# Pooled attention with a frequency mix on one core: the maxima row as a 128x32 product, the tail maxima's last columns at the second burst, and a new order of the first pair

## The chip, the core and the metric

The kernel runs on one core of a Trainium2 chip. The metric is device microseconds of one execution. Engines are named as in the profile: PE (TensorE), DVE (VectorE), ACT (ScalarE), POOL (GpSimd), SP (SyncE, which issues most transfers); PEld is PE's loading of stationary tiles.

## The reference

Inputs: `q`, `k`, `v` of 8 batches x 8 heads x 1152 rows x 64, and four weights. Cut to what is computed:

```python
q_pool = q.reshape(B, H, S // 2, 2, D).mean(axis=3)
scores = scale * q_pool @ k^T
attn = exp(scores - rowmax(scores)); attn = attn / (rowsum(attn) + 1e-9)
x = (attn @ v), heads side by side             # 8 x 576 x 512
theta = x @ w_theta
y = w_tok_r @ (x * cos(theta)) + w_tok_i @ (x * sin(theta))
u = x + y
out = u + max(u @ w_ch, 0)
```

## The kernel before, in words

Two heads are one pair; 32 pairs run one after the other, and then 8 batches of the second phase (theta, cosine and sine, token mix, channel mix).

For each pair, `q` and `k` are loaded (`load_q`, `load_k`, L468 and L478), neighbouring q rows are added (`pool_q`, L484), turned on DVE (`turn_q`, `turn_k`), and split into a rounded part `hi` and a rest `lo`. Pair 0 has its own way: `load_first` (L449) and `first_prep` (L532) turn on PE and copy out of PSUM. A first pass over the pair (`maxpass`, L578) multiplies only the rounded parts, in 12 blocks `pm`, named by two digits (`pm_00` to `pm_32`), each reduced on DVE to row maxima (L599). The last 64 pooled rows of both heads, the tail, take a product of their own with 128x128 tiles: 128 columns in one of the 12 blocks (L596, the block that TAIL_IN names) and 1024 columns in `max_tail` (`px`, L612). `max_nm` folds the maxima (L624), `max_row` (L626) turns them into 9 rows on PE, `max_copy` and `load_max` bring them to the operand `nmr`.

Then 18 score blocks (`escore`, L656), two halves u of 9 K tiles: eight products `pe` in 64x128 tiles, and an exponential on ACT into a buffer `pc`. POOL adds the `pc` tiles up (`ssum`, L679). Two bursts per pair (`burst`, L765) multiply `pc` with `v` (`av`, L702, tile `pa`, 128x64 tiles). The first burst ends with the maxima row of the next pair and the row sums of the last (`norm_sum`, L725, 128x32 tiles); the second begins with `max_tail` for the pair after next.

PSUM has four double banks. `bank2` hands out the one that was given back longest ago, so every product waits for the reader of the block that had its bank before.

The order on every engine is written out by hand. Each step has a position, 18 for each pair and one for each score block, from the tables at the top of the file (EARLY for pairs 0 to 2, MAX_AT0 to MAX_AT2 for their maxima, PLAN, AV_AT and others for the rest, X0_DN and X0_SC for the first batch's normalisation, and for the second phase positions of 56 for each batch, SC1_AT and STORE_LAG among them). The steps are sorted by position, and each engine runs its instructions in that order. `xscale` (L247) multiplies a quarter of x with the reciprocal sums that `dload` brought; `xload` brings x back from memory (DRAM); `zrest` (L402) is the subtraction that gives a rest Z; `fstore` (L1202) writes results out; `xnload` (L263) brings rows of x.

Of the kernel before, what the change touches and what calls it, by code (L numbers as in the profile page):

```python
# [10 lines left out]
F32 = mybir.dt.float32  # L11
F32R = mybir.dt.float32r
# [3 lines left out]
ALU = mybir.AluOpType  # L16
# [4 lines left out]
SHORT = (2, 3, 5, 7, 9, 11, 15, 16, 17, 21, 23, 28, 30)  # L21
REST = (3, 6, 9, 12, 15, 18)
WHOLE = ()
WARM = 16
AGAIN = ((3, 3, 3, 3, 3, 3, 3, 3, 3, 5, 3, 3), (3, 2, 1, 1, 1, 1, 1, 1, 1, 1, 1, 1))
PC_BUFS = 14
MAX_A = ((-23.16, -21.04, -20.44, -19.56, -18.24, -16.98), (-23.16, -21.62, -20.02, -18.45, -18.24, -16.98))
# [3 lines left out]
G_AT = 3.88  # L31
SS_LAG = 6.079
AV_AT = (10.348, 19.269)
AV_AT0 = (10.348, 19.269)
# [4 lines left out]
ROUND1 = (-21.9, -21.8, -21.7)  # L39
LOADV = (-58.9, 11)  # L40
TAIL_IN = (3, 2)
EARLY = {
    0: dict(load_first=-70, first_prep=-60, tail=-25.8, round_lo=-25.75, max=-20.5),
    1: dict(load_k=-69.5, load_q=-69, pool_q=-59, turn_k=-59.5, turn_q=-23.8, tail=-21.65, round_lo=-21.6, max=10.35),
    2: dict(load_k=-58.96, load_q=-58.95, pool_q=-1.0, turn_q=10.31, turn_k=10.32, round_hi=10.5, tail=10.51, round_lo=13.2),
    3: dict(load_k=10.4, load_q=-0.95),
}
MAX_AT0 = (-25.7, -25.2, -24.7, -24.2, -23.7, -23.2, -22.7, -22.2, -21.9, -21.5, -21.4, -21.3)
MAX_AT1 = (-17.75, -17.7, -16.7, -15.7, -14.7, -13.7, -12.7, -11.7)
MID = ((0, 0, 0), (0, 0, 2),(0,0,4),(0,0,6))  # L50
MAX_AT2 = (-22.5, -21.7, -21.1, -19.5, -18.5, -16.8, -15.5, -13.5, -12.5, -10.5, -9.5, -7.8)
HALF_AT = (-21.6, -21.45)
NM_AT = (0.2, 13)
ROW_AT = (0.7, 13)
# [69 lines left out]
def pooled_attention_moe_kernel(  # L124
# [291 lines left out]
    with ExitStack() as p1:  # L416
# [115 lines left out]
        def first_prep(i):  # L532
            st = state[i]
            raw = st["kb"] = opd.tile([P, S + SQ], F32, tag="lo", name="raw0")
            prep(0)
            qx = [st["qn"][0:QP, :, x].rearrange("p t h d -> p t (h d)") for x in range(2)]
            qp = qx[0]
            nc.vector.tensor_tensor(qp, qx[0], qx[1], ALU.add)
            ta, tb = bank2("pta"), bank2("ptb")
            for t in range(KT):  # L540
                dst = ta[:, t // 4, t % 4 * P : (t % 4 + 1) * P] if t < 8 else tb[:, 0, 0:P]
                nc.tensor.transpose(
                    out=dst, in_=st["kn"][:, t].rearrange("p h d -> p (h d)"), identity=ident
                )
# [3 lines left out]
            parts = (
                (ta.rearrange("p b (t f w) -> p (b t) f w", f=32, w=4), 0, 8),
                (tb[:, 0, 0:P].rearrange("p (t f w) -> p t f w", f=32, w=4), 8, 9),  # L550
                (tb[:, 0, P:].rearrange("p (t f r) -> p t f r", t=4, r=3), 0, 4),
                (tb[:, 1, 0 : 2 * QP].rearrange("p (t f r) -> p t f r", t=2, r=3), 4, 6),
            )
# [53 lines left out]
        def max_tail(i):  # L607
            st = state[i]
            hi, tl = st["hi"], st["tail"]
            pm = st["px"] = bank2(f"px{i}")  # L610
            for n in range(2):
                nc.tensor.matmul(  # L612
                    pm[:, n], tl, hi[:, 512 * n : 512 * (n + 1)], start=True, stop=True
                )
        def max_tail_red(i):
            st = state[i]
            mx = st["mx"]
            nc.vector.tensor_reduce(mx[:, 8, 0:2], st["px"], AX.X, ALU.max)
            done(f"px{i}")
# [436 lines left out]
    with ExitStack() as p2:  # L1056
# [157 lines left out]
        for b in range(B):  # L1214
# [104 lines left out]
```

## Time and profile before

| | us |
|---|---|
| median of 3 runs | 1275.29 |
| lowest and highest | 1274.76, 1275.31 |
| the profiled execution | 1278.34 |
| its span, first to last instruction | 1276.6 |
| mean granted TensorE clock | 0.991 of full |

The profile comes from one execution. Busy time and span are read against each other; the granted clock is 1.00 at 2.4 GHz and 0.50 at 1.2 GHz. A timeline row has start, duration, engine, line, operation, output and inputs with the number of instructions merged into it, and in square brackets the idle time of the engine before it with what ended that.

### The profile page before, as it was taken

The numbers are of one execution on the slowest core, as the hardware profiler recorded it, in microseconds if no ns is written. First come the engines' busy times: TensorE is split into PE (matmuls) and PEld (weight loads), VectorE is DVE, ScalarE is ACT, GpSimd is POOL, SyncE is SP. The second block draws the span as 40 slices with busy tenths as digits, with TensorE's granted clock in tenths as the row PEclk, the third lists the DMA queues.
The fourth block names the chain that finished last, engine by engine and source line by source line (L and its number), as shares of the span: only waits on it lengthen the run. The fifth ranks groups of instructions, "written<-read, shape, count | busy, mean of one in ns | idle before, by whom it ended". The sixth has DMA issues, their size and how long they took to land.

```text
span 1276.6 us, 29050 instructions
## 1 busy us (share of the span) xinstructions
PE 1246.7 (98%) x11556; PEld 1006.2 (79%) x11556; DVE 903.5 (71%) x1173; ACT 696.2 (55%) x1241; POOL 854.1 (67%) x581
## 2 busy tenths in 40 slices
PE   7999999999999999999998999989999999999998
PEld 6677776777777777677776777679999999998998
DVE  5787777877778787788886885486675757657642
ACT  3577576666757667666765566554333433334320
POOL 4799899899899979999998887432423514242410
PEclk8999999999999999999999999989999999999999
DMA  9564565566446456565637511126554464555421
GB/s 125 97 124 99 112 120 78 121 110 106 97 96 120 89 122 102 95 127 97 115 69 157 92 44 45 52 71 179 93 139 89 118 148 82 123 95 136 87 38 38
DMA packets 468660, 129.09 MB, mean 101 GB/s; under 512 B 438390, under 2 KB 438780, under 8 KB 468524
## 3 DMA queue, kind: packets, MB, share of 16 engines
q1 hardware_dynamic: 465728, 126.03, 49.7%
q8 instruction: 91, 1.49, 0.5%
q10 hardware_dynamic: 2572, 0.86, 0.3%
q0 software_dynamic: 224, 0.33, 0.1%
q14 instruction: 45, 0.37, 0.1%
HBM read 96.58 MB, written 29.55 MB: 99 GB/s over the span
## 4 chain that ended last, share of the span: by engine, by line
PE 76%; DVE 5%; DMA 5%; POOL 4%; SPq 4%; ACT 3%; issue 3%; ACTq 0%; DVEq 0%; POOLq 0%
PE pe L673 22%; PE pa L708 20%; PE pf L1099 13%; PE pf L1146 5%; PE pf L326 5%; PE pm L587 4%; POOL ss L688 4%; PE pn L737 3%; ACT pc L676 2%; DMA dn<-rd 2%; PE px L612 2%; SPq L463 1%; DVE xT L250 1%; SPq L1207 1%; DMA xs<-dn 1%
## 5 line engine op out<-in xcount | busy, mean ns | idle before, releaser
L688 POOL TENSOR_TENSOR ss<-ss,pc 128x576 f32<-128x576 f32 x346 | 531.2, 1535 | 50.4 <-ACT pc L676 27.8
L599 DVE TENSOR_REDUCE mx<-pm 128x2 f32<-128x768 f32 x384 | 353.1, 952 | 148.1 <-PE pm L587 144.9
L676 ACT ACTIVATE pc<-pe 128x576 f32<-128x576 f32 x576 | 350.3, 651 | 64.4 <-PE pe L673 35.2
L708 PE MATMUL pa<-pc,vn 128*64 128x288 f32 x2304 | 294.4, 409 | 0.0
L708 PEld LDWEIGHTS pa<-pc,vn 128*64 128x64 f32 x2304 | 159.4, 137 | 116.1 <-issue 7.3
L1099 PE MATMUL pf<-wtk,Z 128*128 128x288 f32 x1728 | 234.9, 296 | 4.4 <-DVE Z L406 3.5
L1099 PEld LDWEIGHTS pf<-wtk,Z 128*128 128x128 f32 x1728 | 232.6, 189 | 6.4 <-DVE Z L406 3.7
L406 POOL TENSOR_TENSOR Z<-ab,Z 128x512 fp32r<-128x512 f32 x35 | 47.1, 1347 | 265.9 <-ACT Z L400 228.1
L673 PE MATMUL pe<-hi 64*128 64x288 f32 x1152 | 198.4, 340 | 6.0 <-DVE mx L599 4.6
L673 PE MATMUL pe<-hi,lo 64*128 64x288 f32 x1152 | 170.9, 292 | 0.0
L673 PE MATMUL pe<-lo,hi 64*128 64x288 f32 x1152 | 170.9, 293 | 0.0
L673 PE MATMUL pe<-nmr,oner 64*128 64x288 f32 x1152 | 170.4, 291 | 0.0
L673 PEld LDWEIGHTS pe<-hi 64*128 64x128 f32 x1152 | 108.3, 184 | 60.3 <-issue 27.6
L587 PE MATMUL pm<-hi 64*128 64x384 f32 x826 | 134.5, 349 | 4.7 <-ACT hi L558 1.6
L720 ACT COPY xu<-pa 128x288 f32<-128x288 f32 x64 | 25.5, 399 | 186.5 <-PE pa L708 153.7
L673 PEld LDWEIGHTS pe<-lo,hi 64*128 64x128 f32 x1152 | 109.6, 186 | 0.0
L673 PEld LDWEIGHTS pe<-hi,lo 64*128 64x128 f32 x1152 | 109.1, 185 | 0.0
L673 PEld LDWEIGHTS pe<-nmr,oner 64*128 64x128 f32 x1152 | 109.0, 185 | 0.0
L1146 PE MATMUL pf<-us,wch 128*128 128x288 f32 x768 | 105.4, 296 | 0.9 <-DVE uT L1113 0.9
L1146 PEld LDWEIGHTS pf<-us,wch 128*128 128x128 f32 x768 | 104.0, 188 | 2.8 <-issue 1.3
L688 POOL TENSOR_TENSOR ss<-pc,pc 128x576 f32<-128x576 f32 x62 | 100.7, 1624 | 0.4 <-ACT pc L676 0.4
L587 PEld LDWEIGHTS pm<-hi 64*128 64x128 f32 x826 | 79.4, 191 | 9.7 <-DVE mx L599 2.5
(165 smaller groups left out, 1476.3 us busy)
## 6 DMA issues: line engine op xcount, KB each, us to landing
vn<-in_v_dram SPq DMA_DIRECT2D x128, 144.0 KB
kn<-in_k_dram SPq DMA_DIRECT2D x124, 144.0 KB
qn<-in_q_dram SPq DMA_DIRECT2D x124, 144.0 KB
xd<-xu SPq DMA_DIRECT2D x32, 288.0 KB
xT<-xd SPq DMA_DIRECT2D x8, 1152.0 KB
out_dram<-ot SPq DMA_DIRECT2D x112, 72.0 KB
xn<-xs SPq DMA_DIRECT2D x31, 256.0 KB
dn<-rd SPq DMA_DIRECT2D x32, 160.0 KB
```

The costliest lines, as they stand in the source:

```text
L326: nc.tensor.matmul(th, xs[:, c, j * P : (j + 1) * P], ws[:, c], start=(n == 0), stop=(n == 11))
L406: eng.tensor_tensor(Z[1], t, Z[0].bitcast(F32), ALU.subtract)
L587: nc.tensor.matmul(pm[:, h, 0:W], hi[hs, Q0 + j * P : Q0 + (j + 1) * P], hi[hs, g * W : (g + 1) * W], start=True, stop=True,)
L599: nc.vector.tensor_reduce(mx[:, j : j + 5 : 4, g : g + 1], pm[:, :, 0:W], AX.X, ALU.max)
L612: nc.tensor.matmul(pm[:, n], tl, hi[:, 512 * n : 512 * (n + 1)], start=True, stop=True)
L673: nc.tensor.matmul(pe[:, h, 0:HALF], w[hs], x[hs], start=(n == 0), stop=(n == 3))
L676: nc.scalar.activation(pcs[u, kt], pe[:, :, 0:HALF], AF.Exp, scale=SC)
L688: nc.gpsimd.tensor_tensor(st["ss", u], first, st["pc"][u, kt], ALU.add)
L708: nc.tensor.matmul(pa[hs, 0, 0:HALF], st["vn"][:, h, kt, :], st["pc"][u, kt][:, h, :], start=(kt == 0), stop=(kt == KT - 1),)
L737: nc.tensor.matmul(px[a : a + 32, 1, 0:HALF], ones, sets[u][n][:, h, :], start=(n == 0), stop=(n == len(sets[0]) - 1), tile_position=(0, a),)
L1099: nc.tensor.matmul(st["py", c, u][:, 0:HALF], Z[zi][:, c * P : (c + 1) * P], wtk[wi][:, kw, u * HALF : (u + 1) * HALF], start=(i == 0 and ...
L1146: nc.tensor.matmul(st["pr", e][u][:, 0:HALF], wch[wi][:, c, e * P : (e + 1) * P], st["us", ui, c // 2][:, c % 2, u * HALF : (u + 1) * HALF ...
```

## The change

`max_row` becomes an ordinary product with a tile position; in the second burst `pa`'s bank is taken after `px`'s; the tail's 128 columns move from block `pm_32` to block `pm_12`, which stands before `max_tail`. Pair 0's loads, copies and order are written anew, pair 0's v comes in one transfer, and 11 instead of 16 warm-up products run. Positions around the end of the attention phase and of the stores move. The core of the diff, the tables cut to the lines that the prediction speaks of:

```diff
-WARM = 16
+WARM = 11
-TAIL_IN = (3, 2)
+TAIL_IN = (1, 2)
 EARLY = {
-    0: dict(load_first=-70, first_prep=-60, tail=-25.8, round_lo=-25.75, max=-20.5),
-    1: dict(load_k=-69.5, load_q=-69, pool_q=-59, turn_k=-59.5, turn_q=-23.8, tail=-21.65, round_lo=-21.6, max=10.35),
+    0: dict(load_first=-70, first_prep=-60, tail=-28.757, round_lo=-29.225, max=-20.74),
+    1: dict(load_k=-65.772, load_q=-66.05, pool_q=-27.673, turn_k=-21.464, turn_q=-22.174, tail=-19.658, round_lo=-2.892, max=10.879),
...
-X0_DN = (0.1, 0.2, 9.3, 18.3)
-X0_SC = (6.088, 15.05, 25.552, 42.088)
+X0_DN = (0.1, 0.2, 15.2, 23.2)
+X0_SC = (13.05, 21.05, 30.05, 42.088)
-SC1_AT = -8.365
+SC1_AT = -7.9
-STORE_LAG = 3.237
+STORE_LAG = (3.237, 3.237, 13.0, 13.0)
...
         def load_first():
             kn = vnp.tile([P, KT, 2, D], F32, tag="vn", name="kn0")
-            qn = inp.tile([P, QT, 2, 2, D], F32, tag="qn", name="qn0")
-            for h in range(2):
-                nc.sync.dma_start(kn[:, :, h], k[0, h].rearrange("(p t) d -> p t d", t=KT))
-                nc.scalar.dma_start(
-                    qn[0:QP, :, :, h], q[0, h].rearrange("(p t x) d -> p t x d", t=QT, x=2)
-                )
+            qn = inp.tile([P, 2, QT, 2 * D], F32, tag="qn", name="qn0")
+            ksrc = k[0, 0:2].rearrange("h (p t) d -> h p t d", t=KT)
+            qsrc = q[0, 0:2].rearrange("h (f r t x) d -> r f h (t x d)", r=3, t=QT, x=2)
+            qdst = [qn[32 * r : 32 * r + 32].rearrange("f h t y -> f h (t y)") for r in range(3)]
+            nc.sync.dma_start(kn[:, :, 0], ksrc[0])
+            nc.scalar.dma_start(qdst[0], qsrc[0])
+            nc.sync.dma_start(kn[:, :, 1], ksrc[1])
+            nc.scalar.dma_start(qdst[1], qsrc[1])
+            nc.sync.dma_start(qdst[2], qsrc[2])
...
             for dst in (st["hi"], raw):
-                kd_ = dst[:, 0:S].rearrange("p (t w f) -> p t f w", t=KT, w=4)
-                qd_ = dst[:, Q0:].rearrange("p (r t f) -> p t f r", r=3, t=QT)
-                for n, (src, t0, t1) in enumerate(parts):
-                    nc.scalar.copy((kd_, qd_)[n // 2][:, t0:t1], src)
+                qd_ = dst[:, Q0:].rearrange("p (r t f) -> p t r f", r=3, t=QT)
+                for n, (src, sl) in enumerate(parts):
+                    to = dst[:, sl] if n < 2 else qd_[:, sl]
+                    if n and dst is not raw:
+                        nc.vector.tensor_copy(to, src)
+                    else:
+                        nc.scalar.copy(to, src)
...
         def max_row(i, px):
-            nc.tensor.transpose(out=px[0:KT, 1, 0:P].bitcast(F32R), in_=state[i]["nm"], identity=identr)
+            nc.tensor.matmul(
+                px[0:KT, 1, 0:P], state[i]["nm"], identr, start=True, stop=True, tile_position=(0, 0)
+            )
...
         def burst(i, u):
-            pa = bank2(f"pa{i}_{u}")
             whole_sum(i - 1 + u, 1 - u)
             if u == 0:
-                av(i, u, pa)
+                av(i, u, bank2(f"pa{i}_{u}"))
                 if i > 0:
                     norm_sum(i - 1, bank2(f"pn{i}"))
             else:
                 if i + 2 < NPAIR:
                     max_tail(i + 2)
+                pa = bank2(f"pa{i}_{u}")
+                if i + 2 < NPAIR:
                     max_tail_red(i + 2)
                 av(i, u, pa)
...
             for e in range(0 if last else ND):
                 at2(base + FLIP_AT[e], flip, b, e)
-                at2(base + FLIP_AT[e] + STORE_LAG, fstore, b, e)
+                at2(base + FLIP_AT[e] + STORE_LAG[e], fstore, b, e)
```

Line numbers of the changed kernel are larger by 2 to 16. Three places of the order, first PE at the two bursts. `pm_32` is the last score block of a pair's maxima, `pa_0` the first burst's tile. Before:

```order
1217 L673 MATMUL pe_11_4314<-nmr_146,oner 128x288 x2
1218 L587 MATMUL pm_31_4325<-hi_3941 128x384 x2
1219 L587 MATMUL pm_32_4329<-hi_3941 128x384 x2
1220 L596 MATMUL pm_32_4329<-hi_3941,tail_151 128x128
1221 L708 MATMUL pa_0_4337<-pc_00_4130,vn_4092 64x288 x2
```

Now, at the same burst:

```order
1218 L688 MATMUL pe_11_4310<-nmr_146,oner 128x288 x2
1219 L600 MATMUL pm_31_4321<-hi_3937 128x384 x2
1220 L600 MATMUL pm_32_4325<-hi_3937 128x384 x2
1221 L723 MATMUL pa_0_4331<-pc_00_4124,vn_4086 64x288 x2
1222 L723 MATMUL pa_0_4331<-pc_01_4138,vn_4086 64x288 x2
```

and at the second burst of that pair, where `pm_12` was followed by `px` directly:

```order
1284 L600 MATMUL pm_12_4514<-hi_4304 128x384 x2
1285 L609 MATMUL pm_12_4514<-hi_4304,tail_150 128x128
1286 L625 MATMUL px_4527<-hi_4304,tail_150 128x512 x2
1287 L723 MATMUL pa_1_4530<-pc_10_4292,vn_4086 64x288 x2
1288 L723 MATMUL pa_1_4530<-pc_11_4309,vn_4086 64x288 x2
```

The product with the tail has gone from behind `pm_32` to between `pm_12` and `px`. The second place is DVE at the first scaling of batch 0's x (`xT`), in pairs 26 and 27. Before:

```order
609 L624 TENSOR_REDUCE nm_10388<-mx_10084 128x9
610 L574 TENSOR_TENSOR lo_10362<-kb_10181,hi_10361 128x1728
611 L250 TENSOR_TENSOR xT_10281<-xT_10281,dn_0_10284 128x640
612 L599 TENSOR_REDUCE mx_10458<-pm_00_10459 128x2
613 L599 TENSOR_REDUCE mx_10458<-pm_01_10489 128x2
```

Now:

```order
612 L637 TENSOR_REDUCE nm_10382<-mx_10078 128x9
613 L587 TENSOR_TENSOR lo_10358<-kb_10175,hi_10357 128x1728
614 L612 TENSOR_REDUCE mx_10451<-pm_00_10452 128x2
615 L612 TENSOR_REDUCE mx_10451<-pm_01_10479 128x2
616 L612 TENSOR_REDUCE mx_10451<-pm_02_10499 128x2
617 L612 TENSOR_REDUCE mx_10451<-pm_10_10528 128x2
618 L612 TENSOR_REDUCE mx_10451<-pm_11_10532 128x2
619 L250 TENSOR_TENSOR xT_10277<-xT_10277,dn_0_10280 128x640
```

The scaling moved behind five reductions of the next pair. The third place is DVE at the start of the second phase, where `Z_7` is a rest that batch 0's token mix needs and `xT`, `dn` and `xl` belong to batch 1. Before:

```order
725 L375 TENSOR_TENSOR ti<-xn,ti 128x512
726 L250 TENSOR_TENSOR xT_12342<-xT_12342,dn_0_12351 128x576 x2
727 L250 TENSOR_TENSOR xT_12342<-xT_12342,dn_2_12356 128x576 x2
728 L406 TENSOR_TENSOR Z_7_12497<-ti,Z_7_12496 128x512
729 L270 STREAM_TRANSPOSE dn_0_12351<-xT_12342 128x512 x2
```

Now:

```order
728 L375 TENSOR_TENSOR ti<-xn,ti 128x512
729 L406 TENSOR_TENSOR Z_7_12491<-ti,Z_7_12490 128x512
730 L250 TENSOR_TENSOR xT_12336<-xT_12336,dn_0_12345 128x576 x2
731 L250 TENSOR_TENSOR xT_12336<-xT_12336,dn_2_12350 128x576 x2
732 L270 STREAM_TRANSPOSE dn_0_12345<-xT_12336 128x512 x2
```

`Z_7` stands ahead of the four scalings now.

## Rows read from the trace of the kernel before

**Rows 1.** The page, busy us of each engine, share of the span, instructions.

```profile
PE 1246.7 (98%) x11556; PEld 1006.2 (79%) x11556; DVE 903.5 (71%) x1173; ACT 696.2 (55%) x1241; POOL 854.1 (67%) x581
```

**Rows 2.** Timeline, the start: start us, us, engine line op out<-in, count [idle].

```profile
9.39 1.94 ACT L558 CAST hi<-pta 128x1024 fp32r<-128x1024 f32 x1 [5.55 <-PE pta L542]
12.26 1.33 PE L587 MATMUL pm<-hi 64*128 64x384 f32 x12 [1.60 <-ACT hi L558]
13.29 1.38 DVE L518 STREAM_TRANSPOSE kb<-kn 128x1152 f32<-128x1152 f32 x1 [3.27 <-DMA kn<-in_k_dram]
14.59 3.52 DVE L599 TENSOR_REDUCE mx<-pm 128x2 f32<-128x768 f32 x4
...
19.16 0.78 DVE L522 STREAM_TRANSPOSE kb<-qp 128x576 f32<-128x576 f32 x1 [1.05 <-POOL qp L489]
...
26.24 0.96 DVE L599 TENSOR_REDUCE mx<-pm 128x2 f32<-128x768 f32 x1 [0.85 <-PE pm L587]
...
28.67 1.21 DVE L618 TENSOR_REDUCE mx<-px 128x2 f32<-128x1024 f32 x1
```

**Rows 3.** Timeline of PE, the first burst of pair 13.

```profile
363.47 0.33 PE L596 MATMUL pm<-hi,tail 128*128 128x128 f32 x1
363.73 4.59 PE L708 MATMUL pa<-pc,vn 128*64 128x288 f32 x36
368.25 0.23 PE L627 MATMUL pa<-identr,nm 128*9 128x128 f32 x1
368.40 0.69 PE L737 MATMUL pn<-ss,ones 128*32 128x288 f32 x8
```

**Rows 4.** Timeline of PE, pair 0's first burst, entered from a score block.

```profile
39.23 0.29 PE L673 MATMUL pe<-nmr,oner 64*128 64x288 f32 x2
...
39.45 0.71 PE L708 MATMUL pa<-pc,vn 128*64 128x288 f32 x4
```

**Rows 5.** Timeline, PE and DVE at the second burst of pair 12.

```profile
351.62 0.34 PE L587 MATMUL pm<-hi 64*128 64x384 f32 x2
...
352.01 0.73 PE L612 MATMUL px<-hi,tail 128*128 128x512 f32 x2
...
349.11 2.68 DVE L599 TENSOR_REDUCE mx<-pm 128x2 f32<-128x768 f32 x3
```

**Rows 6.** DVE's timeline in pairs 26 and 27; busy time, clock and DMA by stretch.

```profile
685.58 3.14 DVE L574 TENSOR_TENSOR lo<-kb,hi 128x1728 fp32r<-128x1728 f32 x1
694.21 0.83 DVE L250 TENSOR_TENSOR xT<-xT,dn 128x640 f32<-128x640 f32 x1 [5.49 <-DMA nmr<-mT]
...
699.09 1.82 DVE L599 TENSOR_REDUCE mx<-pm 128x2 f32<-128x768 f32 x2 [1.16 <-PE pm L587]
...
670.40:723.79 53.39, 49.57 (x523) 36.70 (x522) 38.56 (x40) 29.11 (x55) 47.57 (x32) 0.97 0.64 130
723.79:772.96 49.17, 48.79 (x530) 35.38 (x529) 36.98 (x40) 28.95 (x54) 40.58 (x27) 1.00 0.25 58
```

**Rows 7.** Timeline and stretch at the second phase's start (PE, PEld, DVE, ACT, POOL, clock).

```profile
856.11 6.06 PE L1099 MATMUL pf<-wtk,Z 128*128 128x288 f32 x28 [3.47 <-DVE Z L406]
...
858.39 2.45 DVE L305 TENSOR_TENSOR xl<-xT,xh 128x512 fp32r<-128x512 f32 x4
...
856.10:860.40 4.30, 4.29 (x18) 4.29 (x19) 4.30 (x8) 0.01 (x1) 0.00 (x0) 0.50 0.50 78
```

**Rows 8.** Waits over the span: us in total, times, longest us.

```profile
DVE kk L383 <- DMA xn<-xs: 5.3, 2, 3.3
...
ACT pc L676 <- POOL ss L688: 3.5, 10, 1.3
...
PEld px L612 <- ACT pc L676: 10.9, 30, 0.4
```

**Rows 9.** Transfers between 2.4 and 7.4 us.

```profile
DMA packets 4484, 1.13 MB, mean 227 GB/s; under 512 B 4484, under 2 KB 4484, under 8 KB 4484
```

**Rows 10.** The stretch of pair 21, columns as in rows 6 and 7.

```profile
546.20:570.40 24.20, 24.08 (x266) 17.63 (x262) 19.37 (x23) 17.28 (x32) 23.65 (x16) 1.00 0.64 109
```

More of the change, by code (lines that the diff above doesn't have):

```diff
@@ L33 @@
 AV_AT = (10.348, 19.269)
-AV_AT0 = (10.348, 19.269)
+AV_AT0 = (10.997, 19.1)
 W_SLOTS = ((2.7077, 'F'), (2.7082, 'G'), (9.553, 'G'), (9.5535, 'S'), (10.1975, 'G'), (10.3446, 'T'), (10.3451, 'A'), (10.8111, 'D'), (10.975, 'D'), (19.0577, 'F'), (19.0582, 'D'), (19.0587, 'D'))
@@ L38 @@
 POOL_V = (5, 6, 11, 13, 15, 19, 20, 22, 28, 31)
-ROUND1 = (-21.9, -21.8, -21.7)
-LOADV = (-58.9, 11)
-TAIL_IN = (3, 2)
+ROUND1 = (-21.726, -20.451, -15.632)
+LOADV = (-60.841, 10.654)
+TAIL_IN = (1, 2)
 EARLY = {
-    0: dict(load_first=-70, first_prep=-60, tail=-25.8, round_lo=-25.75, max=-20.5),
-    1: dict(load_k=-69.5, load_q=-69, pool_q=-59, turn_k=-59.5, turn_q=-23.8, tail=-21.65, round_lo=-21.6, max=10.35),
-    2: dict(load_k=-58.96, load_q=-58.95, pool_q=-1.0, turn_q=10.31, turn_k=10.32, round_hi=10.5, tail=10.51, round_lo=13.2),
-    3: dict(load_k=10.4, load_q=-0.95),
-}
-MAX_AT0 = (-25.7, -25.2, -24.7, -24.2, -23.7, -23.2, -22.7, -22.2, -21.9, -21.5, -21.4, -21.3)
-MAX_AT1 = (-17.75, -17.7, -16.7, -15.7, -14.7, -13.7, -12.7, -11.7)
+    0: dict(load_first=-70, first_prep=-60, tail=-28.757, round_lo=-29.225, max=-20.74),
+    1: dict(load_k=-65.772, load_q=-66.05, pool_q=-27.673, turn_k=-21.464, turn_q=-22.174, tail=-19.658, round_lo=-2.892, max=10.879),
+    2: dict(load_k=-55.676, load_q=-63.943, pool_q=-4.606, turn_q=7.314, turn_k=8.538, round_hi=9.549, tail=11.548, round_lo=10.935),
+    3: dict(load_k=10.803, load_q=-9.799),
+}
+MAX_AT0 = (-27.018, -25.789, -25.538, -24.906, -24.391, -22.506, -22.456, -22.091, -21.99, -21.491, -21.3, -21.113)
+MAX_AT1 = (-22.101, -17.248, -16.865, -15.788, -14.814, -13.69, -12.081, -8.94)
 MID = ((0, 0, 0), (0, 0, 2),(0,0,4),(0,0,6))
[L51 to L54, printed above, removed]
+MAX_AT2 = (-21.234, -20.605, -19.611, -18.864, -17.2, -16.832, -15.264, -11.416, -10.736, -9.135, -7.866, -7.72)
+HALF_AT = (-21.576, -21.125)
+NM_AT = (-20.052, 11.601)
+ROW_AT = (1.049, 13.548)
 PLAN = {
@@ L494, in load_v @@
             vn = vnp.tile([P, 2, KT, D], F32, tag="vn", name=f"vn{i}")
+            if i == 0:
+                src = v[b, h0 : h0 + 2].rearrange("h (p t) d -> p h (t d)", t=KT)
+                nc.sync.dma_start(vn.rearrange("p h t d -> p h (t d)"), src)
             src = v[b, h0 : h0 + 2].rearrange("h (f w t) d -> w f h (t d)", w=4, t=KT)
-            for w in range(4):
+            for w in range(4 if i else 0):
                 dst = vn[32 * w : 32 * w + 32].rearrange("f h t d -> f h (t d)")
@@ L535, in first_prep @@
             prep(0)
-            qx = [st["qn"][0:QP, :, x].rearrange("p t h d -> p t (h d)") for x in range(2)]
-            qp = qx[0]
-            nc.vector.tensor_tensor(qp, qx[0], qx[1], ALU.add)
+            qx = [st["qn"][0:QP].rearrange("p h t (x d) -> x p t h d", x=2)[x] for x in range(2)]
+            qp = inp.tile([P, QT, 2, D], F32, tag="kb", name="qp0")
+            nc.vector.tensor_tensor(qp[0:QP], qx[0], qx[1], ALU.add)
             ta, tb = bank2("pta"), bank2("ptb")
@@ L546, in first_prep @@
                 dst = tb[:, t // 4, (t // 4 == 0) * P + t % 4 * QP :][:, 0:QP]
-                nc.tensor.transpose(out=dst, in_=qp[:, t], identity=ident[0:QP, 0:QP])
+                nc.tensor.transpose(
+                    out=dst,
+                    in_=qp[0:QP, t].rearrange("p h d -> p (h d)"),
+                    identity=ident[0:QP, 0:QP],
+                )
             parts = (
[L549 to L552, printed above, removed]
+                (ta.rearrange("p b c -> p (b c)"), slice(0, 8 * P)),
+                (tb[:, 0, 0:P], slice(8 * P, S)),
+                (tb[:, 0, P:].rearrange("p (t r f) -> p t r f", t=4, r=3), slice(0, 4)),
+                (tb[:, 1, 0 : 2 * QP].rearrange("p (t r f) -> p t r f", t=2, r=3), slice(4, 6)),
             )
             for dst in (st["hi"], raw):
-                kd_ = dst[:, 0:S].rearrange("p (t w f) -> p t f w", t=KT, w=4)
-                qd_ = dst[:, Q0:].rearrange("p (r t f) -> p t f r", r=3, t=QT)
-                for n, (src, t0, t1) in enumerate(parts):
-                    nc.scalar.copy((kd_, qd_)[n // 2][:, t0:t1], src)
+                qd_ = dst[:, Q0:].rearrange("p (r t f) -> p t r f", r=3, t=QT)
[5 more added lines that the diff above has]
+                        nc.scalar.copy(to, src)
             done("pta")
@@ L626, in max_row @@
         def max_row(i, px):
-            nc.tensor.transpose(out=px[0:KT, 1, 0:P].bitcast(F32R), in_=state[i]["nm"], identity=identr)
+            nc.tensor.matmul(
+                px[0:KT, 1, 0:P], state[i]["nm"], identr, start=True, stop=True, tile_position=(0, 0)
+            )
         def max_copy(i, px):
```

## The prediction

> **What bounds the kernel now.** I read the page's busy shares first. TensorE (PE) is busy 98% of the span, and no other engine over 71% [rows 1]. So time falls only where PE's own row of work gets shorter or where one of its few stops goes. I then looked for both. The timeline of the start shows PE held by ScalarE's copies and VectorE (DVE) busy with the wrong thing [rows 2]. The timeline of one burst shows what a change of tile shape on PE costs [rows 3 to 5]. The stages around the end of the attention phase show two stops, at 692 and at 852 us [rows 6, 7]. Last I read the lists of waits [rows 8].
>
> The profiled execution took 1278.34 us (span 1276.6), 3.05 above the median of the runs shown, 1275.29. The savings below are read in the profiled execution and taken off the median unchanged.
>
> **Start of pair 0.** The first loads move 1.13 MB at 227 GB/s, all of it in packets under 512 B [rows 9]; half of that, 2.5 us, is q. Now q comes in runs of 3072 B. I take 0.6 us (ends: nothing, and half of q's time, 1.25). The first score block begins at 12.26, released by ScalarE, whose first copy alone took 1.94 with a scattered destination [rows 2]. Now the copies are contiguous or nearly so, and three of the four `hi` copies go to DVE. They still wait for q's transposes, so I take 0.5 (ends: nothing, 1.2). DVE spent 13.29 to 14.67 on pair 1's K transposition before it could begin the maxima at 14.59 [rows 2]. Without that they could begin when the first six products are done, at about 12.95 (half of a row of 1.33 that starts at 12.26). That is 1.6 us; the 1.38 is put back later in the same row of DVE work, so 0.2 stays. Between 14.59 and the end of the last reduction at 29.88 DVE stood idle 1.05 (for pooled q of pair 1 from POOL) and 0.85 (for PE) [rows 2], and another 0.40 that I leave out. The new order puts that q transposition three reductions later, and puts the eleventh block of maxima ahead of the small product that waits for the half row; I count 1.7 of the 1.9 as gone. Sum 3.0 us. POOL now subtracts `lo` of pair 0 before it pools q; that is no cost as long as the pooled q arrives by DVE's new place for it. Ends 0.5 and 4.5: against it stands that in pair 0 the 3 us subtraction for pair 2 is now ahead of the last four maxima of pair 1, and PE's `pm_32` waits for a bank behind them.
>
> **Tail columns moved from the first burst to the second.** In the first burst of a pair PE goes from 64x128 tiles to one 128x128 product (L596), then to 128x64 tiles. The product starts at 363.47 and the first `pa` at 363.73, so 0.26 us pass before `pa` [rows 3]. With the product gone, PE changes directly from 64x128 to 128x64. That change stands in the trace: the last score product starts at 39.23 and `pa` at 39.45, 0.22 us [rows 4], so the direct change is no dearer than the one before the product. Of 32 moved products 1 is in pair 0 (counted with the start) and 10 are followed by 128x128 transposes of a weight tile, which have the same shape as the product; I count nothing for those. 21 x 0.26 = 5.5 us (ends: 21 x 0.18 = 3.8 if the direct change costs 0.08 more; 8.1 if the ten save as much).
>
> In the second burst the product comes in front of `px`, which has its shape and its stationary tile. Before, `px` started 0.39 after the score product [rows 5], and it was waiting for a bank that ScalarE's exponential gives back, 30 times, 10.9 us in all [rows 8]. The change takes `px`'s bank first and `pa`'s second, so `px` gets the bank of an older maximum. In the pair shown DVE is done with that at 349.11 + 2.68 = 351.79, before the old start at 352.01 [rows 5]. So the tail takes the place of a wait. At worst the product starts as late as `px` did and `px` 0.26 after it, which costs 30 x 0.26 = 7.8 us; at best the product starts 0.22 in, as `pa` did at 39.45, and `px` straight behind it, a gain of 30 x 0.17 = 5.1. The truth should lie near 0.22 plus the part of 0.26 that is no change of shape, about where `px` starts now. I take 0. DVE reduces the same number of columns. Only the 0.28 us tail maximum is now ahead of `px`'s, where a 4.6 us burst covers it.
>
> **The maxima row as a 128x32 product.** The transpose starts at 368.25 and the first row sum at 368.40 [rows 3]: 0.15 us, 30 times, 4.5 us in all. It has a shape of its own between 128x64 and 128x32. As a 128x32 product it shares the shape of the sums, but the first sum uses the same 32 columns and must follow it. I take half, 2.3 us (ends 4.5, and a loss of 1.0 if the sums' other three column groups now start later). The Trainium skill, "TensorE: Matmul & The Clock Gate", section "The mechanism", says that a weight load overlaps running products only when the row group differs. All row groups are the same here, so by that rule the first sum's load would still stand open and the whole term would be nearly 0. No row here tells load from drain at 368.25, so the trace neither agrees nor disagrees, and it stays a rival.
>
> **The stop at 692 us.** DVE reached the first scaling of x at 688.7 and stood until 694.21 for its data, and everything behind it on DVE, PE's bank among it, stood too. Pairs 26 and 27 take 53.39 us, the next two 49.17, so 4.2 us are lost, part of it at the lower granted clock (0.97 on the mean) [rows 6]. The scaling now comes five reductions later. In the old trace the fifth ends at 699.09 + 1.82 = 700.91 [rows 6]; less 4.2 that is 696.7, still 2.5 us behind the data. The loads that must wait for it on SP's queue were moved behind it too, one v load ahead of them. I take 4.2 (ends 3.0, 4.8).
>
> **The stop at 852 us.** PE waits 3.47 us until 856.11 for one subtraction on DVE that stands behind four scalings, and then runs 4.30 us at a granted clock of 0.50, the lower level [rows 7]. With the subtraction first, PE goes on at about 852.5. But the scalings, the transposes and the subtractions `xl` follow, and those end some 0.8 us later than 858.39 + 2.45 = 860.84; the next theta product needs them, so PE stops there instead. Theta ended at about 864.8 and would end at 863.0; if the clock falls there once more, all of that is given back. I take 1.2 (ends: 0.5 lost, 3.5 gained).
>
> **Stores.** DVE waits twice, 5.3 us, for `xn` rows that were queued behind eight output stores on SP [rows 8]. The load now goes ahead of them. PE hardly stops there, so I take 0.7 (ends 0, 1.9). The stores end later, but their buffer is not written again for about ten steps. Fewer warm-up products (11 for 16) I cost at nothing, because they end before the loads do.
>
> **Sum.** 3.0 + 5.5 + 0 + 2.3 + 4.2 + 1.2 + 0.7 = 16.9 us: 1278.34 becomes 1261.4, and 1275.29 becomes **1258.4**.
>
> **Rivals.** (a) The row product saves nothing: 1258.4 + 2.3 = 1260.7. For it, the rule above; chance 0.13. (b) PE gets ahead and POOL or DVE becomes the bound, so that what the bursts save (7.8) is taken back: 1266.2. For it, POOL is busy 23.65 of 24.20 us in pair 21 [rows 10]; against it, ScalarE waited for a buffer from POOL only ten times, 3.5 us [rows 8]. Chance 0.10. (c) The new first order stalls in pair 0, on DVE's subtraction ahead of the maxima, and the start gives nothing: 1261.4. Chance 0.14. (d) Slower: `px` waits in every second burst for DVE's maximum of the older block. It decides from 0.65 us per burst (30 x 0.65 = 19.5 us, 16.9 + 2.6), and gives 1278 and more. In the row shown DVE is free 0.2 us before `px` [rows 5], so 0.03. (e) The order does not move what it should and all stays: 1275; 0.02. The forecast has the remaining 0.58.
>
> **Numbers.** A measurement of this kernel can tell about 0.2%, 2.6 us, from no change. (a), (b), (c) and the forecast are all faster by more: 0.95; I move 0.01 of it to no change, for mixtures of bad ends. So faster 0.94, within 0.2% 0.03, slower 0.03. The range takes the forecast's ends (8 us below, if bursts, row and start all reach their good ends) and (a) to (c) on the other side: 1251 to 1267.
>
> **What would show it.** Right: the last reduction of pair 0's maxima starting at about 25.7 instead of 28.67; pair length in the middle 24.2 to 24.4 where it was 24.6; in the first burst `pm` then `pa` with 0.2 to 0.3 us between; no stop near 692; PE going on at 852.5. Wrong: PE rows of L625 released by DVE, ScalarE waiting for POOL in many pairs, or a new stop of over 1 us in pair 0.

## The result and the profile after

| | before | changed |
|---|---|---|
| median of 4 runs, us | 1275.30 | 1262.17 |
| lowest and highest, us | 1274.76, 1277.31 | 1262.05, 1263.99 |
| profiled execution, us | 1278.34 | 1263.99 |

The ratio is 0.9898 (95% interval 0.988 to 0.9915): 13.1 us less, where 16.9 were forecast. Runs of one kernel lie up to 5.3 us apart (the kernel before, beside e1 to e4: 1274.71 to 1280.05), so below, a difference of medians under about 3 us is read only together with a trace. The kernel before ran again beside every set of experiments, with medians from 1275.64 to 1276.59; the ratios are taken against these, so the ratios show 0.5 to 1.6 us less than the medians do.

The page of the changed kernel, the line that answers to [rows 1]. PE has lost 6 us of work and is still the bound:

```profile
PE 1240.7 (98%) x11546; PEld 1002.6 (79%) x11546; DVE 900.7 (71%) x1176; ACT 692.0 (55%) x1238; POOL 852.5 (68%) x581
```

Its timeline at the start, for [rows 2]:

```profile
8.98 1.01 ACT L571 CAST hi<-pta 128x1024 fp32r<-128x1024 f32 x1 [6.03 <-PE pta L548]
...
10.77 1.02 DVE L569 CAST hi<-ptb 128x128 fp32r<-128x128 f32 x3 [0.92 <-PE ptb L553]
...
11.67 5.79 PE L600 MATMUL pm<-hi 64*128 64x384 f32 x36 [0.94 <-DVE hi L569]
...
13.04 5.67 DVE L612 TENSOR_REDUCE mx<-pm 128x2 f32<-128x768 f32 x6 [1.25 <-PE pm L600]
...
26.23 1.21 DVE L631 TENSOR_REDUCE mx<-px 128x2 f32<-128x1024 f32 x1
```

The copy takes 1.01 instead of 1.94, the maxima begin at 13.04 instead of 14.59, and the reduction behind `px` comes at 26.23 instead of 28.67. Pair 1's first score product starts at 51.88, 2.71 us earlier than before (54.59).

The first burst of pair 13, for [rows 3]:

```profile
358.16 0.54 PE L600 MATMUL pm<-hi 64*128 64x384 f32 x4
358.63 4.59 PE L723 MATMUL pa<-pc,vn 128*64 128x288 f32 x36
363.15 0.23 PE L640 MATMUL pa<-identr,nm 128*9 128x128 f32 x1
363.30 0.69 PE L752 MATMUL pn<-ss,ones 128*32 128x288 f32 x8
```

The tail product is gone from here. The maxima row still stands 0.15 us ahead of the first sum, as before, and the profile still calls it 128*9.

Two second bursts, for [rows 5], first that of pair 12, then that of pair 16 with DVE's rows:

```profile
347.06 0.33 PE L609 MATMUL pm<-hi,tail 128*128 128x128 f32 x1
347.22 0.68 PE L625 MATMUL px<-hi,tail 128*128 128x512 f32 x2
...
442.69 0.33 PE L609 MATMUL pm<-hi,tail 128*128 128x128 f32 x1
443.07 0.73 PE L625 MATMUL px<-hi,tail 128*128 128x512 f32 x2
443.73 0.46 PE L723 MATMUL pa<-pc,vn 128*64 128x288 f32 x2
...
441.19 1.82 DVE L612 TENSOR_REDUCE mx<-pm 128x2 f32<-128x768 f32 x2 [0.32 <-PE pm L600]
```

In pair 12 `px` follows the tail product after 0.16 us. In pair 16 it follows after 0.38, just behind the end of DVE's reduction (441.19 + 1.82 = 443.01), whose bank it has. Of the 29 second bursts after 60 us, 11 look like that of pair 16. They belong to 11 of the 12 pairs in the table LATE (L29), for which some blocks of maxima stand later.

The end of the attention phase: DVE at the first scaling, and the stretch of pairs 26 and 27 for [rows 6], with the columns of rows 6 and 7:

```profile
687.86 1.82 DVE L612 TENSOR_REDUCE mx<-pm 128x2 f32<-128x768 f32 x2 [0.34 <-PE pm L600]
689.60 1.02 DVE L250 TENSOR_TENSOR xT<-xT,dn 128x640 f32<-128x640 f32 x1
...
664.12:713.27 49.15, 48.22 (x522) 35.16 (x520) 35.38 (x39) 28.99 (x55) 47.32 (x32) 1.00 0.70 142
```

The scaling does not wait, and pairs 26 and 27 take 49.15 us instead of 53.39. The start of the second phase, for [rows 7]:

```profile
845.38 1.12 PE L326 MATMUL pf<-wth,xh 128*128 128x512 f32 x4
848.31 2.60 PE L326 MATMUL pf<-wth,xl 128*128 128x512 f32 x4 [1.82 <-DVE xl L305]
850.71 1.91 PE L326 MATMUL pf<-wth,xh 128*128 128x512 f32 x4
...
848.30:853.90 5.60, 5.38 (x17) 3.86 (x18) 4.61 (x10) 1.83 (x3) 0.00 (x0) 0.70 0.75 119
```

The stop of 3.47 us is gone, and as the prediction said PE stops at `xl` instead, 1.82 us, with the granted clock at 0.70 on the mean of the stretch behind it. From the lists of waits, for [rows 8]: the wait of `kk` for `xn` (5.3 us before) has left the list, but `ab` waits for `xn` once, 2.7 us, which it did not before. ScalarE waits less for POOL, and the last line is the wait of `px` for an older maximum.

```profile
DVE ab L375 <- DMA xn<-xs: 2.7, 1, 2.7
...
ACT pc L691 <- POOL ss L703: 1.1, 5, 0.4
...
PEld px L625 <- DVE mx L612: 2.5, 13, 0.3
```

Followed through the trace, the lead over the kernel before is 2.71 us at pair 1, 6.29 at pair 26, 10.51 at pair 28, 11.06 at the first product of the second phase, 12.03 at batch 1, and 14.36 at batch 6, the end of what is gained. Pairs 1 to 25 take 24.49 us on the mean where they took 24.63; the prediction's sign was 24.2 to 24.4.

### The profile page after: what moved, and what is told of

Its sections match the earlier page's. It is cut to its first block, busy times and chain, and to the rows that moved or that the text cites. A ratio compares the mean times of both kernels' runs of the same rounds, so it can differ in the third digit from the quotient of the medians.

```text
span 1262.2 us, 29058 instructions
## 1 busy us (share of the span) xinstructions
PE 1240.7 (98%) x11546; PEld 1002.6 (79%) x11546; DVE 900.7 (71%) x1176; ACT 692.0 (55%) x1238; POOL 852.5 (68%) x581
## 4 chain that ended last, share of the span: by engine, by line
PE 89%; DVE 6%; ACT 2%; DMA 1%; issue 1%; POOL 0%; SPq 0%; ACTq 0%; DVEq 0%; POOLq 0%
PE pe L688 26%; PE pa L723 23%; PE pf L1115 16%; PE pf L1162 7%; PE pf L326 6%; PE pm L600 5%; PE pn L752 3%; DVE mx L612 2%; PE px L625 1%; DVE xT L250 1%; PE pm L609 1%; DMA dn<-rd 1%; ACT pc L691 1%; DMA qn<-in_q_dram 1%; PE pq L326 0%
```

## The experiments

Every kernel starts from the changed one. Medians stand beside its 1262.17, ratios beside its 0.9898 (0.0010 of a ratio is 1.3 us).

**e1_row_back.** The row is a transpose again.

```diff
-            nc.tensor.matmul(
-                px[0:KT, 1, 0:P], state[i]["nm"], identr, start=True, stop=True, tile_position=(0, 0)
-            )
+            nc.tensor.transpose(out=px[0:KT, 1, 0:P].bitcast(F32R), in_=state[i]["nm"], identity=identr)
```

> The changed kernel with the maxima row as a transpose again. Theory: the row product saves nothing, since the first row sum starts 0.158 us after it where it started 0.157 us after the transpose; so 1262.2 us within 0.6. Rival: the 128x32 product saves its half, 2.3 us, or all of it, 4.5 us, and something else in the pairs took it back; then 1264.5 to 1266.7 us and the distance from row to first sum goes from 0.158 to some lower or higher value.

1262.16 us (ratio 0.989, 0.9875 to 0.9905). From row to first sum 0.16 us, from row to the next score product 363.03 - 361.77 = 1.26, in the changed kernel 364.41 - 363.15 = 1.26. The row product saves nothing that runs or rows could show.

```profile
361.77 0.23 PE L640 MATMUL pa<-identr,nm 128*9 128x128 f32 x1
361.93 0.69 PE L750 MATMUL pn<-ss,ones 128*32 128x288 f32 x8
...
363.03 0.41 PE L686 MATMUL pe<-hi 64*128 64x288 f32 x2
```

**e4_row_group3.** The row moves to the columns of the fourth sum.

```diff
+            a = 96 if i > 1 else 0
             nc.tensor.matmul(
-                px[0:KT, 1, 0:P], state[i]["nm"], identr, start=True, stop=True, tile_position=(0, 0)
+                px[a : a + KT, 1, 0:P], state[i]["nm"].bitcast(F32), ident, start=True, stop=True, tile_position=(0, a)
             )
```

> The changed kernel with the maxima row written to partitions 96 to 104 (tile position 0,96), as an unrounded f32 product, so that it shares its columns with the fourth row sum and not with the first. Theory: the 0.158 us between row and first sum are the time in which the row occupies the column group that the first sum needs; now the first three sums start beside it, and 30 x 0.11 to 0.15 = 3.3 to 4.5 us go: about 1258 to 1259 us, if the unrounded product is not much longer. Rival: all column groups share the row group, so the first sum's load waits for the row whatever its columns: 1262 us, and later if the unrounded product takes longer, up to 30 x 0.2 = 6 us, 1268 us.

1263.89 us (0.9907, 0.9892 to 0.9922). Neither theory holds as it was put:

```profile
362.73 0.28 PE L641 MATMUL pa<-ident,nm 128*9 128x128 f32 x1
362.73 0.11 PEld L759 LDWEIGHTS pn<-ss,ones 128*32 128x32 f32 x1
362.73 0.44 PE L759 MATMUL pn<-ss,ones 128*32 128x288 f32 x3
362.84 0.27 PE L641 MATMUL pa<-ident,nm 128*9 128x128 f32 x1
362.95 0.65 PE L759 MATMUL pn<-ss,ones 128*32 128x288 f32 x5
...
364.01 0.40 PE L695 MATMUL pe<-hi 64*128 64x288 f32 x2
```

Three sums start beside the row, so the first sum did wait for its columns only. But the next score product comes 364.01 - 362.73 = 1.28 us after the row, as late as before. The four sums are equally long, so the one that shares the row's columns ends last, wherever the row stands. The test is not a clean one: unrounded, the row is two products, and the fourth sum starts 362.95 - 362.73 = 0.22 us after it, where a sum follows the rounded row after 0.16. By these numbers I estimate that a rounded row in this place would gain 0.04 us a pair, about 1.3 us in all; no run shows it. The pairs 1 to 25 take the same time to 0.1 us. In the profiled execution the loss comes from a stop of 1.81 us at 1154.72, in front of a theta product; for the other three runs it isn't shown.

**e2_tail_back.** The 128 tail columns return to `pm_32`.

```diff
-TAIL_IN = (1, 2)
+TAIL_IN = (3, 2)
```

> The changed kernel with the tail's 128 columns back in block pm_32, ahead of the first burst. Theory: in pairs 1 to 25 the first bursts got shorter by 0.22 us each whether a weight transpose follows or not, the second ones longer by 0.05, so undoing it costs 30 x 0.16 = 4.9 us: about 1267 us. Rival 1: the pairs got shorter by something else (the row product, a better order of the maxima), then under 1 us. Rival 2: px, without the tail product ahead of it, waits for DVE in all second bursts, then the cost is over 6.5 us.

1265.55 us (0.9919, 0.9903 to 0.9936), 3.4 more than the changed kernel and than e1, which ran beside it; its pairs 1 to 25 are 2.49 us longer. The first burst of pair 13:

```profile
357.59 0.55 PE L600 MATMUL pm<-hi 64*128 64x384 f32 x4
358.06 0.33 PE L609 MATMUL pm<-hi,tail 128*128 128x128 f32 x1
358.32 1.92 PE L723 MATMUL pa<-pc,vn 128*64 128x288 f32 x14
```

From the four `pm` products to `pa` 358.32 - 357.59 = 0.73 us, without the tail 0.47 [358.16 to 358.63 above]. Over the 25 first bursts of these pairs the path through the tail to the next product is 12.82 us long and the direct one 7.27. Up to `pa` it saves 0.24 on the mean of the 15 without a weight transpose behind `pm`, and 0.17 on the mean of the ten with one: 0.13 in eight, and 0.33 in pairs 24 and 25, whose transposes are not 128x128 but in the tiles of the score products. Pairs 6 and 25 of the changed kernel:

```profile
187.27 0.66 PE L897 MATMUL pwt<-ident,ws 128*128 128x128 f32 x4
...
652.92 0.43 PE L897 MATMUL pwt<-ident,ws 64*128 64x64 f32 x4
```

All 25 together save 5.3 us, and 6.6 with pairs 26 to 30. In the second bursts the tail costs 0.07 each (from the last `pm` product to `pa` 1.06 without it, 1.13 with it). It costs nothing in the bursts of the table LATE that wait for DVE's older maximum, for they do so without the tail too (about 1.3 us both times), and 0.11 in the others. Net 5.3 - 1.7 = 3.6; the 1.1 us that are missing to the 2.49 stand in three pairs. Pairs 1, 20 and 23 are 0.28, 0.11 and 0.51 longer in the changed kernel than here, pair 23 by one wait of 0.53 us for DVE that e1 has with 0.07. The other 22 are 0.10 to 0.37 shorter.

**e3_pa_first.** `pa` takes its bank ahead of `px` again, the tail stays.

```diff
-                if i + 2 < NPAIR:
-                    max_tail(i + 2)
                 pa = bank2(f"pa{i}_{u}")
                 if i + 2 < NPAIR:
+                    max_tail(i + 2)
                     max_tail_red(i + 2)
```

> The changed kernel with pa's bank taken ahead of px's in the second burst, as in the kernel before; the tail stays at the second burst. px then waits for an exponential on ACT, not for DVE's older maximum. Theory: about ten second bursts lose 0.25 us or more to that maximum (tail product to px 0.24 us on the mean where it is 0.16 without a wait); without it up to 30 x 0.08 = 2.3 us go: 1260 us, and all second bursts are alike. Rival: px waits for the exponential as it did before the change (0.42 us after the score product), the tail product hides in that wait, but pa then waits for the older maximum: no gain, 1262 us. Rival 2: px is later than now in the twenty bursts without a wait: 1263 to 1266 us.

1260.84 us (0.9883, 0.9868 to 0.9898). The second burst of pair 16 now:

```profile
441.68 0.33 PE L609 MATMUL pm<-hi,tail 128*128 128x128 f32 x1
441.85 0.71 PE L625 MATMUL px<-hi,tail 128*128 128x512 f32 x2
442.49 0.46 PE L723 MATMUL pa<-pc,vn 128*64 128x288 f32 x2
```

`px` follows after 0.17 us where it took 0.38. From `pm_12` to `pa` no second burst takes over 1.15 us, where eleven took 1.27 to 1.52, and pairs 1 to 30 are 1.14 us shorter. From the last `pm` product to `pa`, the second bursts of pairs 1 to 29 take 31.40 us before, 33.10 in the changed kernel and 31.41 here. So with the old order the tail product fills the wait for the exponential and costs nothing, and the new order of the banks was a loss of 1.7 us, not a part of the gain. The medians and ratios point the same way, but their intervals overlap.

**e5_start_back and e5_code_back.** The first has pair 0's loads, copies and all positions of pairs 0 to 2 as before, the second only the loads (L454 to L459, L498) and copies (L564 to L571).

```diff
-WARM = 11
+WARM = 16
...
-    0: dict(load_first=-70, first_prep=-60, tail=-28.757, round_lo=-29.225, max=-20.74),
+    0: dict(load_first=-70, first_prep=-60, tail=-25.8, round_lo=-25.75, max=-20.5),
...
-                    if n and dst is not raw:
-                        nc.vector.tensor_copy(to, src)
-                    else:
-                        nc.scalar.copy(to, src)
+                    nc.scalar.copy((kd_, qd_)[n // 2][:, t0:t1], src)
```

> The changed kernel with pair 0's loads and copies, v's load, the 16 warm-up products and all positions of pairs 0 to 2 as before the change. Theory: the new start is worth what pair 1's first score shows, 2.7 us in the profiled run of the change and up to 4 in the three others that began their maxima at the full clock; so 1265 to 1266 us and pair 1 at about 54.5. Rival: half of it is the tail's move, which also changed pair 0, then under 1.5 us, 1263.5.

1264.84 us (0.9908, 0.9893 to 0.9923). Pair 1's first score product starts at 52.78; in the ten profiled kernels with the whole new start it starts between 50.09 and 51.88. By these rows the new start is worth 0.9 to 2.7 us, 2.0 by the mean of the ten; the medians say 2.7 and the ratios 1.3. The rival isn't ruled out: between the kernel before (54.59) and this one lie another 1.8 us with the same start, from the tail's move or from the clock, which was 0.51 between 24.5 and 31.4 us before and 1.00 here. No run separates the two.

> The changed kernel with only the loads of q, k and v of pair 0 and the copies after its transposes as before; the positions and the 11 warm-up products stay new. Theory: loads 0.6 and copies 0.5 us were the smaller part of the start; 1263.3 us, first maximum product 1.1 us later, at about 12.4. Rival: the order is only possible with the early copies, and the whole 2.7 us go: 1265 us. Rival 2: the copies' gain hides behind DVE, which is busy from 13 us on, then 1262.2.

1265.33 us (0.9915, 0.99 to 0.993), no better than with the old order too, and pair 1 starts at 54.93:

```profile
9.90 1.93 ACT L558 CAST hi<-pta 128x1024 fp32r<-128x1024 f32 x1 [6.05 <-PE pta L542]
...
12.76 2.82 PE L587 MATMUL pm<-hi 64*128 64x384 f32 x14 [1.45 <-ACT hi L558]
...
14.13 0.96 DVE L599 TENSOR_REDUCE mx<-pm 128x2 f32<-128x768 f32 x1 [3.96 <-PE pm L587]
```

ScalarE's copies hold everything, and DVE stands idle 3.96 us ahead of the first reduction, a part of which the old order filled with pair 1's K. So the order alone gains nothing; it needs the short copies. The 54.93 is not the price of the copies alone, for the granted clock was 0.50 from 8.87 to 19.11 us in this execution. That the copies' gain hides behind DVE, the second rival, is wrong.

**e6_x0_back.** The first scaling of x as before.

```diff
-X0_DN = (0.1, 0.2, 15.2, 23.2)
-X0_SC = (13.05, 21.05, 30.05, 42.088)
+X0_DN = (0.1, 0.2, 9.3, 18.3)
+X0_SC = (6.088, 15.05, 25.552, 42.088)
```

> The changed kernel with X0_DN and X0_SC as before. Theory: the first scaling of x again stands on DVE ahead of the maxima of pair 27 and waits for its data; PE stops 3.65 us near 690 us and two pairs take 4.2 us more: 1266.4 us. Rival: the data come earlier now, or PE has work to fill it, then under 2 us: 1264.

1266.58 us (0.992, 0.9903 to 0.9936), 4.4 more by the medians and 2.8 by the ratios. Pairs 26 and 27 take 53.98 us where the changed kernel takes 49.15, and the stop is back:

```profile
685.27 1.76 DVE L250 TENSOR_TENSOR xT<-xT,dn 128x640 f32<-128x640 f32 x1 [6.01 <-DMA dn<-rd]
...
687.96 0.61 PE L688 MATMUL pe<-hi 64*128 64x288 f32 x2 [4.25 <-DVE mx L612]
```

**e7_sc1_back.** The rest Z_7 behind the four scalings.

```diff
-SC1_AT = -7.9
+SC1_AT = -8.365
```

> The changed kernel with SC1_AT back at -8.365, so that batch 1's four scalings stand ahead of batch 0's rest Z_7 on DVE again. Theory: PE stops about 3.5 us before the first product of the second group instead of 1.82 us before the theta product with xl, both times with a half clock after it; the difference of the two is the 1.0 us that the traces differ by: 1263.2 us. Rival: the two stops are worth the same, 1262.2. Rival 2: the old stop costs its whole length more, 3.5 us: 1265.7.

1263.71 us (0.9901, 0.9887 to 0.9914), 1.5 more by the medians and 0.4 by the ratios, which is not clear of the noise. The old stop is back, of the same length as in [rows 7]:

```profile
844.01 5.50 PE L1115 MATMUL pf<-wtk,Z 128*128 128x288 f32 x28 [3.47 <-DVE Z L406]
...
844.00:848.30 4.30, 4.29 (x21) 4.29 (x22) 4.30 (x8) 0.01 (x1) 0.00 (x0) 0.60 0.50 78
```

From batch 0's first token mix product to batch 1's it takes 58.86 us here and 59.43 before, in the eleven kernels with the new order and theta as it was 57.1 to 58.6. What the change gains here hangs on the granted clock after the stop that is left: in eight of the eleven it is 0.82 on the mean of the 9.3 us behind the stop (58.1 to 58.6 us), in e1, e2 and e10 it stays at 1.00 (57.1 us), with the same stop of 1.82 to 1.83 us.

**e8_lag_back.** All stores of a batch as early as before.

```diff
-STORE_LAG = (3.237, 3.237, 13.0, 13.0)
+STORE_LAG = (3.237, 3.237, 3.237, 3.237)
```

> The changed kernel with all four stores of a batch 3.237 positions behind their transpose, as before. Theory: DVE waits twice for rows of x that stand behind stores on SP, and PE's sum of the second phase is longer by the 2.15 us that the traces of before and of the change differ by between batches 4 and 6: 1264.3 us. Rival 1: my estimate, 0.7 us: 1262.9. Rival 2: a stop near 1155 us comes and goes by itself (one run of the changed order had one of 1.8 us, with a half clock after it), and the lag is worth nothing: 1262.2.

1263.75 us (0.99, 0.9885 to 0.9915), 1.6 more by the medians and 0.3 by the ratios, so only the trace can tell. Between batches 4 and 6 it is 0.74 us longer than e1's. There is a stop of 0.32 us in front of the channel mix, which before the change took 0.94 and which no trace with the new lag has, and one of 0.70 in front of a theta product, where the changed kernel has 0.34. The wait of DVE's `kk` for `xn` is back once (2.7 us). So my estimate, 0.7, is the nearest. What the other 1.4 of the 2.15 us between the traces of before and of the change are stays open. The stop in front of theta can come without the old lag: e4, with the new one, lost 3.03 us there.

```profile
1139.08 2.19 PE L1162 MATMUL pf<-us,wch 128*128 128x288 f32 x15 [0.32 <-DVE uT L1129]
...
1152.21 1.19 PE L326 MATMUL pf<-wth,xh 128*128 128x512 f32 x4 [0.70 <-DVE r L354]
```

Before the change, the first of the two:

```profile
1155.33 1.96 PE L1146 MATMUL pf<-us,wch 128*128 128x288 f32 x13 [0.94 <-DVE uT L1113]
```

**e9_row64.** As e3, with the row as two 64x128 products behind the sums.

```diff
+            for n, hs in enumerate(HEADS):
+                nc.tensor.matmul(px[:, n, 320:384], nmw[hs], identr[hs, hs], start=True, stop=True)
```

> As e3 (pa's bank first), and the maxima row is made by two 64x128 products behind the row sums instead of one 128x9 product ahead of them: two halves of the maxima by two halves of the identity, each with 64 columns, into the sums' bank; the maxima stand in a tile of 128 columns. Theory: the row's 0.158 us are the time of a product that nothing runs beside; in the shape of the score products that follow, the two run beside each other and cost 0.06 to 0.12; 30 x 0.04 to 0.10 = 1.2 to 3 us go: 1258 to 1259.5 us where e3 took 1260.8. Rival: a change of operands costs the same in any shape: 1260.8. Rival 2: the row is 1.2 us later, so nmr lands after the first score products of the next pair want it: over 1263.

1285.56 us (1.0074, 1.0061 to 1.0088), the worst of all, for two reasons that are no test of the theory. The identity is made in another way, by DVE, and the first product waits for it (9.8 us); pair 0 starts 5.99 us later than in e3. And the row, in the sums' bank, waits for ScalarE to have read the sums:

```profile
PEld pn L649 <- ACT sm L768: 34.7, 30, 1.2
...
377.40 0.30 PE L649 MATMUL pn<-identr,nmw 64*128 64x64 f32 x2 [0.62 <-ACT sm L768]
377.54 0.38 PE L697 MATMUL pe<-hi 64*128 64x288 f32 x2
```

With 30 x 0.62 = 18.6 and 6.0 us both are accounted for. The row itself takes 0.13 to 0.14 us in this shape, so by that I estimate that at best 30 x 0.03 us were to be had, below the theory's range.

**e10_warm16.** As e3, with 16 warm-up products.

```diff
-WARM = 11
+WARM = 16
```

> As e3, with 16 warm-up products as before the change instead of 11. With 11, PE is idle 1.0 to 1.6 us ahead of the first transposes, and in four of the runs with the new start that were profiled so far (the changed kernel, e3, e4 and one more) the clock was at its half level in the first maxima, 13 to 15 us, in others not. Theory: with the gap closed the clock stays at the full level until 15 us, as in the runs that had luck, and pair 1 begins at about 50.3 to 50.5: up to 1.3 us less where the fall is avoided, 1260 us. Rival: the fall has another cause (PE waits again at 9.7 and 11.4 us): no difference to e3, 1260.8, and the clock falls as often.

1261.48 us (0.9881, 0.9867 to 0.9894), as e3. The clock falls here too: granted 0.63 between 11 and 15 us, and pair 1 starts at 50.79. The theory fell: the longer warm-up did not hold the clock in this execution. Among the ten kernels with the new start the clock of these 4 us was 1.00 (2.4 GHz) in four and on the mean 0.50 (1.2 GHz) to 0.66 in six, of which two have 16 warm-up products.

**e11_combined.** As e10, with the term that holds `xl` last in theta (L324).

```diff
-        for xs, ws in ((st["xh"], wth[0]), (st["xl"], wth[0]), (st["xh"], wth[1])):
+        for xs, ws in ((st["xh"], wth[0]), (st["xh"], wth[1]), (st["xl"], wth[0])):
```

> As e10 (pa's bank first, 16 warm-up products), and in every theta product the term with xl comes last of the three instead of second. The stop of 1.82 us at 848 us waits for DVE's xl; four products of the other term, 0.95 us by the row at 860.70, now run ahead of it. Theory: the stop falls to about 0.9 us and the clock after it falls less often: 1 to 2 us less than e10, about 1260 us, and faster than the kernel before and the changed one. Rival: xl comes with the clock already low and the time is given back: 1261.5 us.

1260.68 us (0.9877, 0.9857 to 0.9898), the best ratio, but not clear of e3 and e10, and its interval overlaps the changed kernel's.

```profile
841.61 2.04 PE L326 MATMUL pf<-wth,xh 128*128 128x512 f32 x8
844.54 2.30 PE L326 MATMUL pf<-wth,xl 128*128 128x512 f32 x4 [0.89 <-DVE xl L305]
...
847.80:857.10 9.30, 9.29 (x58) 9.29 (x59) 4.86 (x8) 4.73 (x8) 0.42 (x1) 0.82 0.72 179
```

The stop falls from 1.82 to 0.89 us as expected. But in this profiled execution PE then runs at a granted clock of 0.82, where e10's ran at 1.00, and the rival's loss comes: batch 1 starts 0.98 us later than in e10, though the first product behind theta was 1.07 us earlier, of which 0.54 were there before the stop. How often that falls so is open.

## Why the prediction was right, and where its terms were wrong

The time came inside the range and on the right side, 3.8 us above the forecast. Term by term:

| term | forecast | measured | by |
|---|---|---|---|
| start of pair 0 | 3.0 | 2.0 (0.9 to 2.7), clock not separated | e5_start_back |
| tail out of the first burst | 5.5 | 6.6 (30 bursts) | e2_tail_back |
| second burst: tail and bank order | 0 | a loss of 1.7, of the bank order | traces, e3_pa_first |
| maxima row | 2.3 | 0.0 | e1_row_back |
| stop at 692 us | 4.2 | 4.2 to 4.8 | traces, e6_x0_back |
| stop at 852 us | 1.2 | 1.0 (0.3 to 1.8) | traces, e7_sc1_back |
| stores | 0.7 | 0.7 | trace of e8_lag_back |

**Right.** The mechanism held: PE stayed the bound (98% busy), its row of work got shorter at the first burst, and the stops named went. The 3.8 us are mostly the row (2.3), the second burst (1.7) and the start (1.0), less 1.1 that the first burst gave more. The two stops went as worked out, the second one with the new stop at `xl` that was named. The sum for the first burst came near by errors that offset each other. It took 0.26 for 21 bursts and nothing for ten. Those without a weight transpose save 0.24 each, though the direct change of tile shape costs 0.06 more than the one behind the product (0.32 to 0.26 on the mean). The ten with one save 0.17 on the mean, and in two of them the transposes do not have the shape that the prediction gave them. That the term came within 1.1 us is luck in part.

**The row.** The step "it shares the shape of the sums", so half of 0.15 us is saved, failed: the first sum starts 0.16 us after the row in either form, and rival (a), that the row saves nothing, was right. The Trainium skill, "TensorE: Matmul & The Clock Gate", section "The mechanism", says that a weight load overlaps running products only when the row group differs. The trace of e4 does not agree: three sums, loads included, start within 0.02 us of the row in the same row group. So the rival's outcome came, but not for that reason. In e4 what runs one after the other is what shares columns, and since all four column groups carry equal work, the row delays one of them wherever it stands, by 0.16 us rounded and 0.22 unrounded. With the row at nothing and the second burst a loss, a pair in the middle gained 0.14 us, where the forecast's 5.5 + 2.3 = 7.8 over 30 pairs is 0.26.

**The second burst.** The step "I take 0" had the row of a pair in which DVE was done 0.2 us earlier. In 11 of the 12 pairs of the table LATE it isn't. That is the mechanism of rival (d), in 11 bursts of 29: from the last `pm` product to `pa` they take 14.44 us where they took 11.73, 2.7 more, about a seventh of the 19.5 that rival needed to decide. The other 18 take 1.0 less. e2 and e3 show that the change of bank order made the wait, not the tail: without the tail the wait is there as well, and with the old order it is gone. The tail alone did cost nothing, as forecast. The reading from one pair was the fault; the next place to look was the table that treats 12 pairs otherwise.

**The start.** The order of DVE's work was taken to save 1.9 and the loads and copies 1.1. e5_code_back shows that they are not two terms, for without the new loads and copies the new order gained nothing. The six executions whose clock fell between 11 and 15 us show a cost that the sum did not have. With the clock at 1.00 pair 1 starts at 50.1 to 50.5, else at 50.6 to 51.9.

**Rivals (b), (c), (e).** ScalarE waits for POOL 1.1 us in all, less than before; the first burst's gain was not taken back. The start did not stall. Two of the prediction's signs of being wrong did come, both too small to decide: a new stop of 1.42 us at 25.90 behind ScalarE's `hi`, and waits of `px` (L625) for DVE, 2.5 us in all. The terms of the table make 12.8, where the medians fell by 13.1 and the two profiled executions differ by 14.4. Single terms are known to 1 or 2 us at best, so that agreement is no proof of each; what of the start is the clock, and 1.4 us around batch 5, stay open.

## What to carry to other kernels

Count what a product costs by the products that follow it, not by its own shape. Here a small product ahead of four equally long ones, each in columns of its own, delayed one of them wherever it stood. Taking a product out between two others is worth the difference of the two paths, here 0.13 to 0.33 us, by the shapes of the neighbours. Before a bank order is changed, read the wait that it removes and the one that it makes in every kind of pair, above all where a table treats some pairs apart. A scaling or a subtraction that waits for a transfer belongs behind the work of others on its engine.

## What the runs showed of the hardware

A product in another column group starts beside the sums at once (e4, 362.73 both). The clock at the start isn't set by the program alone: with the same instructions up to 15 us it was 1.00 between 11 and 15 us in e1 and 0.64 in e3. With five more products ahead it was 0.63 in both executions (e10, e11). A stop of 0.9 us was followed by a stretch at 0.82 in e11; one of 1.82 us by 0.82 in eight executions and by 1.00 in three.
